# A state-space layer mixed with a feed-forward layer: first loads dealt anew to two queues, six first blocks begun with one row group, x's columns 256 to 447 in one load

## The chip, the cores and the metric

One core of a Trainium2 chip runs the whole program. The metric is device time in microseconds (us). Three runs of the kernel before gave 136.68, 136.72 and 136.97 us, so the median is 136.72. One more execution was recorded by the hardware profiler; it took 136.32 us, of which 134.8 lie between its first and its last instruction (the span). All rows of profiles in this text count from the start of that span.

The engines are TensorE (PE, with its weight loads as PEld), VectorE (DVE), ScalarE (ACT), GpSimd (POOL) and SyncE (SP). SyncE computes nothing here; it issues transfers. ScalarE issues transfers too, in its own queue, between its other instructions. Each engine works through its own instructions in the order in which they were written, and waits on semaphores for others.

## What is computed

```python
x = A_x                                                     # 2048 x 448, bf16
g = sigmoid((x * gate_w).sum(-1, keepdims=True))
# a: a diagonal complex state space with 448 states
Lam_bar = exp(dt * Lam)
Bu = einsum("bld,pd->blp", x, ((Lam_bar - 1) / Lam)[:, None] * Bmat)
h[t] = Lam_bar * h[t - 1] + Bu[t]
a = 2 * einsum("blp,dp->bld", h, Cmat).real + x * Dskip
# b: a feed-forward layer, 448 -> 1792 -> 448
b = silu(x @ w1) @ w2
out = g * a + (1 - g) * b
```

Only the first 9 us or so concern this change: the part of `x @ w1` for the first quarter of the rows.

## The kernel before

**Rows and tiles.** Two neighbouring rows of x are one row of a view `x2` with 1024 rows of 896 columns: columns 0 to 447 are the even row, 448 to 895 the odd one. The work on rows is in four chunks of 512: even rows of the first and second half, then odd rows. Each chunk of `x @ w1` has 14 blocks of 128 columns of w1, and the 448 of the contraction are cut into three parts of 128 (`j` = 0, 1, 2) and a remainder of 64. TensorE needs x transposed, with the contraction along the partitions: that is the tile `XT`, and `XR` holds a copy of a remainder in the other half of the partitions.

**The first chunk is special.** All other chunks are transposed by the transfer engines. The first one, rows 0 to 511 of `x2`, is loaded as it lies into `XH` (a view of the tile `XN`), in four row groups of 128 rows (`k` = 0 to 3), and TensorE transposes it by multiplying with the identity (`turn_k`, line 493; `turn_x` does two row groups). The result stands in a bank of PSUM, and VectorE copies it into `XT` (`turned_k` for one row group, line 503; `turned_x` for two or all four, line 509). The bank of each `j` is in `PB = (6, 7, 6, 7)`; for `j` = 0 the row groups use bank 6, 5, 6 and 7.

**Loads.** Lines 275 to 294 issue them. Columns 0 to 255 of the four row groups are four loads (`XA0` to `XA3`, 64 KB each). W1's first part (`j` = 0, the first 768 columns of w1) is two loads of 384 columns (`W1Ej00`, `W1Ej01`, 96 KB each), the second and third part one load of 192 KB each (`W1Ej1`, `W1Ej2`). Columns 256 to 383 and 384 to 511 of all four row groups are two loads of 128 KB (`XB0`, `XB1`); of the second, the last 64 columns belong already to the odd rows. The order in the queues is:

| place | SyncE's queue | ScalarE's queue |
|---|---|---|
| 1 | x, row group 0 | x, row group 1 |
| 2 | W1 first part, columns 0 to 383 | W1 first part, columns 384 to 767 |
| 3 | x, row group 2 | x, row group 3 |
| 4 | W1 second part | Lambda_im |
| 5, 6 | log_dt, Lambda_re | x columns 256 to 383; W1 third part |
| 7 | x columns 384 to 511 | (an activation table is loaded) |
| then | W1's remainder and later columns | W1's remainder and later columns |

**The order on TensorE.** It starts with 20 matmuls on constants (`warm`, line 483). Then come the transposes of row groups 0 and 1, and the generator `ffn1_first` (line 424), which computes six blocks (0, 2, 4, 1, 3, 5; even blocks need only the first half of W1's first part) for `j` = 0, 1 and 2 in six banks. It gives up control at each `yield`, and the lines around line 518 put the transposes in these places:

1. three even blocks with row group 0 alone (128 columns, line 427), then the same with row group 1 (line 435);
2. transposes of row groups 2 and 3, `j` = 0;
3. three odd blocks with row groups 0 and 1 (256 columns); transposes of row groups 2 and 3 for `j` = 1;
4. six blocks with row groups 2 and 3 (256 columns); three blocks for `j` = 1 (512 columns);
5. four tiny matmuls that turn the parameter rows into columns (`mm_cols`, line 474);
6. the four transposes for `j` = 2 into bank 6, which VectorE copies out in one piece; three blocks for `j` = 1;
7. the four transposes for the last columns into bank 7; six blocks for `j` = 2;
8. the remainders (`ffn1_rem`, line 449), two blocks side by side in the two halves of the array, each followed by a Silu on ScalarE (line 457).

After it the dense part runs to the end, mainly lines 362, 816, 801 and 1054.

**Who waits for whom.** `Tracker` keeps for each name (such as `ps6` for bank 6, or `XB0`) the last writer and the readers since. A reader waits for the last writer; a writer waits for the last writer and for all readers. A bank is one name, whatever part of it is used:

```python
        for b in writes:
            st = self.state(b)
            if st.w is not None:
                add(*st.w)
            for key, value in st.r.items():
                add(key, value)
```

**On VectorE and ScalarE in this time.** VectorE copies transposes out (lines 503, 509, 573), copies the parameter columns (line 530) and computes decays and phases in small steps (lines 558 to 584); from 10 us on it builds phases (lines 614, 616, 621), spreads two broadcast rows (`GD`, line 672), copies a remainder (line 241) and rearranges B (lines 680, 682). ScalarE computes two exponentials of the parameters (line 564), the second of them from a product that VectorE makes after its copy of `j` = 2; then it loads the table for Silu (line 574) and starts the Silus.

Of the kernel before, what the change touches and what calls it, by code (L numbers as in the profile page):

```python
# [11 lines left out]
BF16 = DT.bfloat16  # L12
# [7 lines left out]
D = 448  # L20
# [130 lines left out]
def gated_mix(nc, A_x, A_Lambda_re, A_Lambda_im, A_B_re, A_B_im, A_C_re, A_C_im, A_log_dt,  # L151
              A_Dskip, B_x, B_w1, B_w2, gate_w, out):
    with ExitStack() as ctx:
        E = ctx.enter_context
        T = Tracker(nc, ctx)
# [15 lines left out]
        XR = sb("XR", [128, NK], BF16)  # L171
# [4 lines left out]
        XN = sb("XN", [128, 2 * NKT * D], BF16)  # L176
# [12 lines left out]
        ID = sb("ID", [128, 128], BF16)  # L189
# [31 lines left out]
        ps = E(nc.psum_tensor("ps", [128, 8, 512], F32))  # L221
# [3 lines left out]
        def ld(eng, dst, src, key, group=None):  # L225
            return T.dma(eng, lambda e: e.dma_start(dst, src), writes=[key], group=group)  # L226
# [2 lines left out]
            return T.dma("sp", lambda e: e.dma_start_transpose(dst, src), reads=reads,  # L229
                         writes=[key, *also], group=group)  # L230

        XE = [(["XTe000", "XTe001", "XTe010", "XTe011", "XTe02"], ["XTe03"]), (["XTe1"], ["XTer1"])]
        XO = [([f"XTo{h}"], [f"XTr{h}"]) for h in range(2)]

        def swap_xr(eng, h, odd):
            hs = slice(h * 512, (h + 1) * 512)
            if odd:
                T.op(eng, lambda e: e.tensor_copy(XR[0:64, hs], XT[64:128, 7, hs]), reads=XO[h][1],
                     writes=[f"XR{h}b"])
            else:  # L240
                T.op(eng, lambda e: e.tensor_copy(XR[64:128, hs], XT[0:64, 3, hs]), reads=XE[h][1],
                     writes=[f"XR{h}a"])
# [8 lines left out]
            return v.rearrange("(o n) -> o n", o=1)  # L251

        XH = XN[:, 0:8 * D].rearrange("p (k c) -> p k c", k=4)
        XA = ["XA0", "XA1", "XA2", "XA3", "XB0", "XB1"]
        FA, FB = 768, 1280
        x0 = x2[0:512, 0:512].rearrange("(k p) c -> p k c", p=128)

        def ld_w(eng, j, f0=0, f1=FA, key=""):
            ld(eng, W1E[:, j, f0:f1], B_w1[j * 128:(j + 1) * 128, f0:f1], f"W1Ej{j}{key}")
# [12 lines left out]
                          B_w1[384:448, FA:].rearrange("p (n c f) -> p n c f", n=2, c=2)[:, :, c, :], f"W1Es{c}")  # L272
            return ld(eng, W1E[p, 3, 0:384], B_w1[384:448, 384 * c:384 * c + 384], f"W1Er{c}")

        for k, eng in enumerate(("sp", "act")):
            ld(eng, XH[:, k, 0:256], x0[:, k, 0:256], XA[k])
        for c, eng in enumerate(("sp", "act")):
            ld_w(eng, 0, 384 * c, 384 * c + 384, c)
        for k, eng in ((2, "sp"), (3, "act")):
            ld(eng, XH[:, k, 0:256], x0[:, k, 0:256], XA[k])  # L280
        ld_w("sp", 1)
        for i, (eng, v) in enumerate((("sp", A_log_dt), ("sp", A_Lambda_re), ("act", A_Lambda_im))):
            ld_row(eng, i, v)
        for i, eng in enumerate(("act", "sp")):
            ld(eng, XH[:, :, 256 + 128 * i:384 + 128 * i], x0[:, :, 256 + 128 * i:384 + 128 * i], XA[4 + i])
        ld_w("act", 2)
        T.op("act", lambda e: e.activation(JK[:, 0:1], HP[:, :], AF.Exp), reads=["HP"], writes=["JK0"])
        gE = [ld_wr(eng, c, False) for c, eng in enumerate(("sp", "act"))]
        ld_w3("sp", 0, 2, FA, FB, "d")
# [8 lines left out]
            ld("act", dst[0:32, :], row(src).partition_broadcast(32).rearrange("p o n -> p (o n)"), key)  # L298

        def load_xn(h):  # L300
            c0 = 0 if h else 512
            ld("sp", XN[:, 8 * h * D:8 * (h + 1) * D].rearrange("p (k c) -> p k c", k=4)[:, :, c0:],
               x2[h * 512:(h + 1) * 512, c0:].rearrange("(k p) c -> p k c", p=128), f"XN{h}")

# [5 lines left out]
        for i, src in enumerate((A_B_re, A_B_im)):  # L310
# [15 lines left out]
             writes=["IOTA"])  # L326
# [19 lines left out]
        def rem_keys(odd, h, p):  # L346
            return (XO if odd else XE)[h][1] if (p is UP) == bool(odd) else [f"XR{h}{'b' if odd else 'a'}"]

# [74 lines left out]

        def ffn1_first():
            banks = [nxt() for _ in range(NF1)]
            for fb in (0, 2, 4):
                T.op("pe", lambda pe, fb=fb, bank=banks[fb]: pe.matmul(
                    ps[:, bank, 0:128], W1E[:, 0, ff(fb) * 128:(ff(fb) + 1) * 128], XT[:, 0, 0:128],
                    start=True, stop=True), reads=["W1Ej00", "XTe000a"], writes=[f"ps{banks[fb]}"])
            for j, h in ((0, 0), (0, 1), (1, None), (2, None)):  # L430
                for n, fb in enumerate((0, 2, 4, 1, 3, 5)):
                    k = h == 0 and n < 3
                    c = slice(0, 512) if h is None else slice(128 if k else 256 * h, 256 * h + 256)
                    bank = banks[fb]
                    T.op("pe", lambda pe, fb=fb, bank=bank, j=j, h=h, c=c, k=k: pe.matmul(  # L435
                        ps[:, bank, c], W1E[:, j, ff(fb) * 128:(ff(fb) + 1) * 128], XT[:, j, c],
                        start=(h == 0 and not k), stop=(h == 0 and not k), skip_group_check=(h != 0 or k)),
                        reads=[f"W1Ej{j}" if j else f"W1Ej0{fb % 2}"] + (
                            ["XTe02"] if j == 2 else [f"XTe0{j}{h}"] if h is not None else [f"XTe0{j}0", f"XTe0{j}1"]),
                        writes=[f"ps{bank}"])  # L440
                    if (j, h, n) in ((0, 0, 2), (0, 0, 5), (1, None, 2), (1, None, 5)):
                        yield
            yield banks

# [34 lines left out]
        def warm(n, b):  # L479
            def mm(pe):  # L480
                ins = None
                for _ in range(n):
                    ins = pe.matmul(ps[:, b, 0:128], ones, ones, start=True, stop=True)
                return ins
            T.op("pe", mm, writes=[f"ps{b}"])
# [3 lines left out]
        xp = [ps[:, b, 0:256].bitcast(BF16) for b in PB]  # L489

        def turn_k(j, k, b=None):
            b = PB[j] if b is None else b
            T.op("pe", lambda pe: pe.transpose(  # L493
                ps[:, b, 0:256].bitcast(BF16)[:, k * 128:(k + 1) * 128], XH[:, k, j * 128:(j + 1) * 128], ID[:, :]),
                reads=[XA[k if j < 2 else 2 + j], "ID"], writes=[f"ps{b}"])

        def turn_x(j, i):
            for k in (2 * i, 2 * i + 1):
                turn_k(j, k)
# [6 lines left out]
        def turned_x(j, i=None, b=None):  # L506
            c, key = (slice(0, 512), f"XTe0{j}") if i is None else (slice(256 * i, 256 * i + 256), f"XTe0{j}{i}")
            b = PB[j] if b is None else b
            T.op("dve", lambda e: e.tensor_copy(XT[:, j, c], ps[:, b, 0:256].bitcast(BF16)[:, c]),
                 reads=[f"ps{b}"], writes=[key])  # L510

        for k in range(2):
            turn_k(0, k, 6 - k)
            turned_k(0, k, 6 - k)
        turn_x(1, 0)
        turned_x(1, 0)
        warm(1, 4)
        first = ffn1_first()
        next(first)
        for k in (2, 3):  # L520
# [3 lines left out]
        for k in (2, 3):  # L524
# [5 lines left out]
        T.op("dve", lambda e: e.tensor_copy(  # L530
            PV[:, :, :], ps[:, 7, 256:288].rearrange("p (t c) -> p t c", c=8)[:, :, 0:4]),
            reads=["pv", "ps7"], writes=["PV"])
        for i in range(2):
            turn_x(2, i)
        turned_x(2)
        next(first)
        for i in range(2):
            turn_x(3, i)
# [8 lines left out]
        def col(n):  # L547
            i = pc(n)
            return P[:, i, :]
# [13 lines left out]
        def pact(o, a, f, ra, scale=1.0, bias=0.0):  # L563
# [5 lines left out]
            col("phf"), LIM, 1.0 / TWO_PI, col("dt"), ALU.mult, ALU.mult), reads=["PV", "dt"], writes=["phf"])  # L569
        ptt("ar", col("dt"), LRE, ALU.mult, ["dt", "PV"])  # L570
        pact("mag", col("ar"), AF.Exp, ["ar"])
        turned_x(3)
        T.op("dve", lambda e: e.tensor_copy(XR[64:128, 0:512], xp[3][0:64, :]), reads=["ps7"], writes=["XR0a"])
        T.op("act", lambda e: e.activation(JK[:, 0:1], HP[:, :], AF.Silu), reads=["HP"], writes=["JK0"])
        ld_b(GWB, gate_w, "GW")
        ld_b(DB, A_Dskip, "DB")
# [9 lines left out]
            reads=["f2"] + SGN, writes=["f2s"])  # L586
        first = next(first)
# [54 lines left out]
        def xblock(b):  # L642
            v = XN[:, 4 * b * D:4 * (b + 1) * D].rearrange("p (k c) -> p k c", k=4) if b > 1 else \
                XH[:, :, b * D:(b + 1) * D]
            return v, [*(XA if b < 2 else []), *([f"XN{b // 2}"] if b else [])]

        def block(tile):
            return tile // 4 if tile > 7 else tile % 2
# [19 lines left out]

        phases(0)
        phases(2, "dve")  # L670
        for n in (32, 64):
            T.op("dve", lambda e, n=n: e.tensor_copy(GD[n:2 * n, :, :], GD[0:n, :, :]), reads=["GW", "DB"],
                 writes=["GW", "DB"])
        phases2(0)
        decays()
        swap_xr("dve", 1, 0)
        phases2(2)
        phases(3)
        phases(1, "dve")
# [1 line left out]
             writes=["BTz"] + BTK[2:4])  # L681
# [486 lines left out]
        f = ffn1(2)  # L1168
# [100 lines left out]
```

## Time and profile before

| | us |
|---|---|
| median of three runs | 136.72 |
| the profiled execution | 136.32 |
| its span | 134.8 |
| TensorE busy in the span | 131.4 |
| VectorE | 115.5 |
| ScalarE | 93.7 |
| GpSimd | 15.9 |
| transfer engines, share of 16, from 0.8 to 4.0 / 4.0 to 6.6 / 6.6 to 9.3 | 0.62 / 0.93 / 1.03 |

The page's 40 slices are 3.37 us each, so the change lies in the first three of them:

```profile
PE   7899999999999999999999999999999999999993
DVE  1379999917999798999999999999999999994554
ACT  0469698899939999769999597796124337879200
POOL 7109358550000000000000000000000000000000
DMA  3999959996994310000211000000000000222123
```

Each digit is the busy share of one slice in tenths. Issuing a transfer is not counted as busy. The waits of TensorE before 14 us, by what ended them (time in all, how often, longest):

```profile
PE ps L427 <- DMA W1E<-in_B_w_dram: 0.4, 1, 0.4
```

On the weight loads there are three more: 0.6 us for the same load, 0.3 us in two pieces for the loads of x (line 493), and 0.2 us for a copy by VectorE (line 503).

### The profile page before, as it was taken

The page shows a single profiled execution, that of the slowest core. Times are in us where ns is not written, and L with a number is a line of the kernel's source. Part 1 is how long each engine was busy: PE and PEld are TensorE (multiplying, and loading weights), DVE is VectorE, ACT ScalarE, POOL GpSimd, SP SyncE. Part 2 cuts the span into 40 slices and gives each one's busy share as a digit, 9 for nine tenths or more (in the row PEclk, how much of TensorE's full clock was granted, in tenths as well). Part 3 has the DMA queues.
Part 4 walks back from the last instruction along what each step waited for, and adds up shares of the span by engine and source line. Part 5 has one row for each costly group of instructions (what it writes and reads, how often), then busy time and mean ns, then how long its engine had stood idle before and what let it go on. Part 6 is the DMA issues. An engine that isn't in the chain of part 4 may idle for free.

```text
span 134.8 us, 2637 instructions
## 1 busy us (share of the span) xinstructions
PE 131.4 (97%) x1074; PEld 65.7 (49%) x1075; DVE 115.5 (86%) x154; ACT 93.7 (70%) x146; POOL 15.9 (12%) x32
## 2 busy tenths in 40 slices
PE   7899999999999999999999999999999999999993
PEld 7544444444444554444445544445555555555552
DVE  1379999917999798999999999999999999994554
ACT  0469698899939999769999597796124337879200
POOL 7109358550000000000000000000000000000000
DMA  3999959996994310000211000000000000222123
GB/s 103 258 284 191 181 129 220 179 379 182 264 188 98 71 46 0 0 0 5 66 45 45 5 0 0 0 5 0 0 0 0 0 0 15 92 94 76 68 81 124
DMA packets 25248, 11.78 MB, mean 87 GB/s; under 512 B 17619, under 2 KB 24726, under 8 KB 25238
## 3 DMA queue, kind: packets, MB, share of 16 engines
q1 hardware_dynamic: 23252, 10.47, 33.4%
q10 hardware_dynamic: 1986, 1.17, 3.0%
q8 instruction: 8, 0.13, 0.4%
q14 instruction: 2, 0.02, 0.0%
HBM read 5.34 MB, written 1.84 MB: 53 GB/s over the span
## 4 chain that ended last, share of the span: by engine, by line
PE 93%; DMA 3%; ACTq 1%; DVE 1%; issue 0%
PE ps L362 44%; PE ps L801 16%; PE ps L816 16%; PE ps L1054 15%; DMA XN<-in_A_x_dram 3%; PE ps L435 1%; ACTq L226 1%; DVE TMPS L1078 1%; PE ps L449 1%; PE ps L493 0%
## 5 line engine op out<-in xcount | busy, mean ns | idle before, releaser
L362 PE MATMUL ps<-XT,W1E 64*128 64x512 bf16 x325 | 41.4, 376 | 0.0
L457 ACT ACTIVATE AT<-ps 128x1024 bf16<-128x1024 f32 x28 | 28.2, 1019 | 7.4 <-PE ps L362 7.2
L362 PEld LDWEIGHTS ps<-XT,W1E 64*128 64x128 bf16 x325 | 16.9, 94 | 19.0 <-ACT AT L457 0.3
L362 PE MATMUL ps<-XT,BT 64*128 64x512 bf16 x156 | 22.4, 377 | 0.0
L816 PE MATMUL ps<-W,AT 64*128 64x448 bf16 x224 | 21.5, 349 | 0.0
L801 PE MATMUL ps<-W,AT 128*128 128x448 bf16 x112 | 21.4, 353 | 0.0
L816 PEld LDWEIGHTS ps<-W,AT 64*128 64x128 bf16 x224 | 10.9, 94 | 10.4
L801 PEld LDWEIGHTS ps<-W,AT 128*128 128x128 bf16 x112 | 10.9, 98 | 10.5 <-issue 0.4
L845 ACT ACTIVATE BT<-ps,GT 128x448 bf16<-128x448 f32 x8 | 5.1, 633 | 13.2 <-PE ps L801 13.2
L901 DVE SCALAR_TENSOR_TENSOR HS<-VE,P,ps 128x512 bf16<-128x512 bf16 (+1 forms) x13 | 9.6, 780 | 3.8 <-PE ps L362 3.8
L362 PEld LDWEIGHTS ps<-XT,BT 64*128 64x128 bf16 x156 | 8.1, 94 | 9.3 <-DVE HS L901 0.4
L945 DVE TENSOR_TENSOR_SCAN G<-P,Q 128x1024 f32<-128x1024 f32 (+1 forms) x6 | 11.4, 1922 | 0.0
L1054 PE MATMUL ps<-CO,VE 128*128 128x448 bf16 (+2 forms) x63 | 11.1, 332 | 0.0
L1054 PE MATMUL ps<-CO,HS 128*128 128x448 bf16 x56 | 11.1, 353 | 0.0
L362 PE MATMUL ps<-XR,W1E 64*128 64x512 bf16 x25 | 9.3, 376 | 0.0
L1054 PEld LDWEIGHTS ps<-CO,VE 128*128 128x128 bf16 x63 | 6.0, 98 | 4.8
L1054 PEld LDWEIGHTS ps<-CO,HS 128*128 128x128 bf16 x56 | 5.5, 98 | 5.1
L898 DVE TENSOR_TENSOR Q<-G,COS 128x2048 bf16<-128x2048 f32 (+1 forms) x4 | 7.0, 1756 | 0.1
L898 DVE TENSOR_TENSOR Q<-G,SIN 128x2048 bf16<-128x2048 f32 (+1 forms) x4 | 7.0, 1751 | 0.0
L863 ACT ACTIVATE VE<-ps 128x1024 bf16<-128x1024 f32 x6 | 6.1, 1019 | 1.2 <-PE ps L362 1.2
L865 ACT ACTIVATE ps<-VE,P 128x1024 f32<-128x1024 bf16 x6 | 6.7, 1118 | 0.2
L901 DVE SCALAR_TENSOR_TENSOR VE<-HS,P,FP 128x512 bf16<-128x512 bf16 (+1 forms) x7 | 6.6, 977 | 0.1
(126 smaller groups left out, 181.2 us busy)
## 6 DMA issues: line engine op xcount, KB each, us to landing
W<-in_B_w_dram SPq DMA_DIRECT2D x2, 784.0 KB, 5.9
XN<-in_A_x_dram SPq DMA_DIRECT2D x1, 896.0 KB, 5.3
out_dram<-OT SPq DMA_DIRECT2D x8, 112.0 KB, 1.7
out_dram<-TMPS SPq DMA_DIRECT2D x7, 112.0 KB, 1.7
HS<-HS SPq DMA_DIRECT2D x4, 128.0 KB, 2.3
XN<-in_A_x_dram SPq DMA_DIRECT2D x1, 384.0 KB, 3.8
W1E<-in_B_w_dram SPq DMA_DIRECT2D x1, 256.0 KB, 5.0
W1E<-in_B_w_dram ACTq DMA_DIRECT2D x1, 256.0 KB, 5.3
```

The costliest lines, as they stand in the source:

```text
L226: return T.dma(eng, lambda e: e.dma_start(dst, src), writes=[key], group=group)
L362: ins = pe.matmul(ps[:, bank, :], w(p, j), xh(odd, h, j, p), start=start and j == js[0], stop=stop and j == js[-1], skip_group_check=seeded)
L457: T.op("act", lambda e: e.activation(a[:, fb:fb + n, :], ps[:, bank:bank + n, :], AF.Silu), reads=[f"ps{bank + i}" for i in range(n)], wri ...
L801: ins = pe.matmul(ps[:, bank, 0:D], a[:, fb, q * 128:(q + 1) * 128], W2[:, ff(fb), :], start=(first and fb == 0), stop=(fb == NFB - 1), sk ...
L816: ins = pe.matmul(ps[:, bank, 0:D], a[p, fb, q * 128:(q + 1) * 128], W2[p, ff(fb), :], start=(start and fb == 0), stop=(not start and fb = ...
L845: T.op("act", lambda e: e.activation(bs(tile), ps[:, bank, 0:D], AF.Copy, scale=sc), reads=[f"ps{bank}", "GT2" if h else "GRI"], writes=ks)
L863: T.op("act", lambda e: e.activation(VE[:, m:m + 2, hs], ps[:, b[0]:b[0] + 2, :], AF.Copy), reads=[f"ps{i}" for i in b], writes=vs)
L865: T.op("act", lambda e: e.activation(ps[:, o[0]:o[0] + 2, :], VE[:, m:m + 2, hs], AF.Copy, scale=c1("lr", pt)), reads=vs + ["lr"], writes= ...
L898: T.op("dve", lambda e: e.tensor_tensor(o, a, b, op), reads=reads, writes=writes)
L901: T.op("dve", lambda e: e.scalar_tensor_tensor(o, a, s, b, ALU.mult, ALU.add), reads=reads, writes=writes)
L945: T.op("dve", lambda e: e.tensor_tensor_scan(G[:, c, w], rb, Q1[:, c, w], init, ALU.mult, ALU.add), reads=[f"Q1{c}", "rr", f"G{c}"], write ...
L1054: ins = pe.matmul(ps[:, bank, c], state(kt, odd, m), CO[:, m, c], start=False, stop=(m == YB[-1]), skip_group_check=True)
```

## The change

It does seven things.

1. Both halves of W1's first part are issued on ScalarE's queue, in places 1 and 2; row groups 0, 1 and 2 of x are places 1 to 3 of SyncE's. Row group 3 stays at place 3 of ScalarE's.
2. Columns 256 to 447 of the four row groups are one load of 192 KB on ScalarE's queue, named `XB` (`XA[4]`), where the load of columns 256 to 383 was. W1's third part moves to SyncE's queue, to the place of the former second load. The 64 columns of odd rows that this load no longer brings come with the later load of that half (`load_xn(0)`, 448 columns instead of 384).
3. The last part's transposes take columns 320 to 447, so that the remainder stands in partitions 64 to 127 of the bank; two copies of 64 partitions bring it to both places.
4. `ffn1_first` begins all six blocks with row group 0, then all six with row group 1, 128 columns each.
5. Row groups 0 and 1 are transposed for `j` = 0 and `j` = 1 as each arrives, with two matmuls on constants in between (one before, after both).
6. For `j` = 1 one block more comes ahead of the transposes for `j` = 2, and these are copied out in two pieces, each after two transposes.
7. On VectorE the first phase step and the copy of the remainder come ahead of the two copies of `GD`.

```diff
-        XA = ["XA0", "XA1", "XA2", "XA3", "XB0", "XB1"]
+        XA = ["XA0", "XA1", "XA2", "XA3", "XB"]
-        x0 = x2[0:512, 0:512].rearrange("(k p) c -> p k c", p=128)
+        x0 = x2[0:512, 0:D].rearrange("(k p) c -> p k c", p=128)
...
-        for k, eng in enumerate(("sp", "act")):
-            ld(eng, XH[:, k, 0:256], x0[:, k, 0:256], XA[k])
-        for c, eng in enumerate(("sp", "act")):
-            ld_w(eng, 0, 384 * c, 384 * c + 384, c)
+        for i in range(2):
+            ld("sp", XH[:, i, 0:256], x0[:, i, 0:256], XA[i])
+            ld_w("act", 0, 384 * i, 384 * i + 384, i)
         for k, eng in ((2, "sp"), (3, "act")):
             ld(eng, XH[:, k, 0:256], x0[:, k, 0:256], XA[k])
         ld_w("sp", 1)
...
-        for i, eng in enumerate(("act", "sp")):
-            ld(eng, XH[:, :, 256 + 128 * i:384 + 128 * i], x0[:, :, 256 + 128 * i:384 + 128 * i], XA[4 + i])
-        ld_w("act", 2)
+        ld("act", XH[:, :, 256:D], x0[:, :, 256:D], XA[4])
+        ld_w("sp", 2)
...
-            c0 = 0 if h else 512
+            c0 = 0 if h else D
...
-            for fb in (0, 2, 4):
+            for fb in (0, 2, 4, 1, 3, 5):
...
-                    start=True, stop=True), reads=["W1Ej00", "XTe000a"], writes=[f"ps{banks[fb]}"])
+                    start=True, stop=True), reads=[f"W1Ej0{fb % 2}", "XTe000a"], writes=[f"ps{banks[fb]}"])
...
-                    k = h == 0 and n < 3
+                    k = h == 0
...
-                    if (j, h, n) in ((0, 0, 2), (0, 0, 5), (1, None, 2), (1, None, 5)):
+                    if (j, h, n) in ((0, 0, 2), (0, 0, 5), (1, None, 2), (1, None, 3), (1, None, 5)):
                         yield
...
             b = PB[j] if b is None else b
+            c = min(j * 128, D - 128)
...
         for k in range(2):
             turn_k(0, k, 6 - k)
             turned_k(0, k, 6 - k)
-        turn_x(1, 0)
+            turn_k(1, k)
+            if k == 0:
+                warm(2, 4)
         turned_x(1, 0)
-        warm(1, 4)
...
+        next(first)
         for i in range(2):
             turn_x(2, i)
-        turned_x(2)
+            turned_x(2, i)
         next(first)
...
-        turned_x(3)
-        T.op("dve", lambda e: e.tensor_copy(XR[64:128, 0:512], xp[3][0:64, :]), reads=["ps7"], writes=["XR0a"])
+        for b, key in ((XT[0:64, 3, 0:512], "XTe03"), (XR[64:128, 0:512], "XR0a")):
+            T.op("dve", lambda e, b=b: e.tensor_copy(b, xp[3][64:128, :]), reads=["ps7"], writes=[key])
...
         phases(0)
         phases(2, "dve")
+        phases2(0)
+        swap_xr("dve", 1, 0)
         for n in (32, 64):
             T.op("dve", lambda e, n=n: e.tensor_copy(GD[n:2 * n, :, :], GD[0:n, :, :]), reads=["GW", "DB"],
                  writes=["GW", "DB"])
-        phases2(0)
         decays()
-        swap_xr("dve", 1, 0)
```

More of the change, by code (lines that the diff above doesn't have):

```diff
@@ L230, in ldt @@
                          writes=[key, *also], group=group)
-        XE = [(["XTe000", "XTe001", "XTe010", "XTe011", "XTe02"], ["XTe03"]), (["XTe1"], ["XTer1"])]
+        XE = [(["XTe000", "XTe001", "XTe010", "XTe011", "XTe020", "XTe021"], ["XTe03"]), (["XTe1"], ["XTer1"])]
         XO = [([f"XTo{h}"], [f"XTr{h}"]) for h in range(2)]
@@ L438, in ffn1_first @@
                         reads=[f"W1Ej{j}" if j else f"W1Ej0{fb % 2}"] + (
-                            ["XTe02"] if j == 2 else [f"XTe0{j}{h}"] if h is not None else [f"XTe0{j}0", f"XTe0{j}1"]),
+                            ["XTe020", "XTe021"] if j == 2 else [f"XTe0{j}{h}"] if h is not None else [f"XTe0{j}0", f"XTe0{j}1"]),
                         writes=[f"ps{bank}"])
-                    if (j, h, n) in ((0, 0, 2), (0, 0, 5), (1, None, 2), (1, None, 5)):
+                    if (j, h, n) in ((0, 0, 2), (0, 0, 5), (1, None, 2), (1, None, 3), (1, None, 5)):
                         yield
@@ L492, in turn_k @@
             b = PB[j] if b is None else b
+            c = min(j * 128, D - 128)
             T.op("pe", lambda pe: pe.transpose(
-                ps[:, b, 0:256].bitcast(BF16)[:, k * 128:(k + 1) * 128], XH[:, k, j * 128:(j + 1) * 128], ID[:, :]),
-                reads=[XA[k if j < 2 else 2 + j], "ID"], writes=[f"ps{b}"])
+                ps[:, b, 0:256].bitcast(BF16)[:, k * 128:(k + 1) * 128], XH[:, k, c:c + 128], ID[:, :]),
+                reads=[XA[k if j < 2 else 4], "ID"], writes=[f"ps{b}"])
         def turn_x(j, i):
@@ L644, in xblock @@
                 XH[:, :, b * D:(b + 1) * D]
-            return v, [*(XA if b < 2 else []), *([f"XN{b // 2}"] if b else [])]
+            return v, XA if b == 0 else [f"XN{b // 2}"]
         def block(tile):
```

## The prediction

> **What bounds the kernel now.** I read first the table of busy time by stretch, to learn whether an earlier start is worth anything at the end. Its columns are the stretch in us, its length, and the busy time and count of PE, weight loads, DVE, ACT and POOL.
>
> ```profile
> 0.80:4.00 3.20, 2.83 (x25) 2.56 (x25) 1.00 (x7) 0.24 (x1) 2.81 (x7) 1.00 0.62 161
> ...
> 6.60:9.30 2.70, 2.54 (x21) 1.27 (x18) 1.83 (x8) 1.64 (x3) 0.00 (x0) 1.00 1.03 298
> 9.30:90.00 80.70, 80.70 (x777) 37.62 (x776) 74.18 (x89) 70.12 (x106) 12.71 (x20) 1.00 0.46 98
> 90.00:132.30 42.30, 42.30 (x231) 22.12 (x228) 36.85 (x46) 20.49 (x37) 0.00 (x0) 1.00 0.12 39
> ```
>
> From 9.3 us on TensorE is busy for all of every stretch. So the moment at which the remainder matmuls of line 449 start (9.31) fixes the end: what that moment gains or loses, the span of 134.8 gains or loses, as long as no new wait appears behind it.
>
> Second, the chain of waits, in order of time: what leads to line 449.
>
> ```profile
> 2.77 4.00 DMA XN<-in_A_x_dram
> 6.77 0.05 issue
> 6.82 0.40 PE ps L493 x4
> 7.21 0.05 issue
> 7.27 0.59 PE ps L435 x2
> 7.86 0.22 PE ps L493 x4
> 8.08 1.29 PE ps L435 x6
> 9.38 0.75 PE ps L449 x6
> 10.13 31.76 PE ps L362 x294
> ```
>
> The chain passes through one load: x's columns 256 to 383, issued on ScalarE's queue at 2.77, landed at 6.77. Behind it TensorE works without a break.
>
> Third, the timeline of the same time: what TensorE did before that load landed, and how long it idled for it.
>
> ```profile
> 4.49 0.34 PE L493 MATMUL ps<-ID,XN 128*128 128x128 bf16 x2
> ...
> 4.75 0.36 DVE L503 COPY XT<-ps 128x128 bf16<-128x128 bf16 x2 [0.88 <-PE ps L493]
> ...
> 5.16 1.48 PE L435 MATMUL ps<-XT,W1E 128*128 128x256 bf16 x9
> ...
> 6.47 0.24 PE L474 MATMUL ps<-ID,R 128*128 128x4 bf16 x4
> ...
> 6.81 0.23 PEld L493 LDWEIGHTS ps<-ID,XN 128*128 128x128 bf16 x4 [0.19 <-DMA XN<-in_A_x_dram]
> 6.82 0.40 PE L493 MATMUL ps<-ID,XN 128*128 128x128 bf16 x4
> 7.25 0.42 DVE L509 COPY XT<-ps 128x512 bf16<-128x512 bf16 x1 [0.32 <-PE ps L493]
> ```
>
> The four small matmuls of line 474 are streamed by about 6.58 (6.47 plus four at 0.028); the transposes start at 6.82. Some 0.24 us of idle time is all that this wait costs. Before it, the six 256-column matmuls that begin at 5.16 wait for row group 3: its load lands at 4.5 (issued 1.72, 2.8 to landing), is transposed, and VectorE copies it out by 5.11.
>
> **The change, part by part.** From start-to-start times here: a warm transpose takes 0.056 us, a 256-column matmul 0.11, a 512-column one 0.215.
>
> *Early loads and first blocks.* Both halves of W1's first block go on ScalarE's queue (0.78 and 1.24, landing before at 1.24 + 2.7 and 1.24 + 2.9), row groups 0 to 2 on SyncE's, row group 3 stays third on ScalarE's. The first matmul can start near 3.6, where it starts now at 4.01. The three 128-column matmuls of odd blocks and three more now stand ahead of the transposes of row groups 2 and 3; they replace three of 256 columns, so the sum of columns is the same. What follows is bound elsewhere: the six 256-column matmuls cannot start until row group 3 has landed plus 0.6 (5.16 - 4.5). Its queue now carries 192 KB ahead of it instead of 160; SyncE's carries 192 KB up to row group 2 instead of 224, and W1's second block then competes sooner. Bounds: 0.2 earlier, since 192 KB of x come with no W1 between them on SyncE's queue and the two landings there now (2.8 and 4.3) lie far apart, or 0.3 later (32 KB more on its own queue and as much from the other, at the 257 GB/s of the stretch from 4.0 to 6.6). I take no shift, start 5.16, range 4.95 to 5.45. From there the order of work up to the wait for columns 256 and on is 0.66 (six of 256) + 0.65 (three of 512) + 0.11 (line 474) + 0.22, since one 512-column matmul more is moved ahead of the wait: 1.64. TensorE is there at 6.80 (6.59 to 7.09).
>
> The row: the 20 warm-up matmuls fill 0.82 to 2.90, 0.105 apart, the same size takes 0.056 at 6.82; what is pulled ahead of about 4.3 runs at half pace. The Trainium skill, "TensorE: Matmul & The Clock Gate", section "Part 1: The HAM clock gate", puts the same down to a gate that opens after some 3.4 us of activity, in a free-running window, and so speaks against this part. By the row a start 0.4 earlier at 4.01 would be worth 0.2 of warm work; by the rule a window that ends later makes it less and changes from run to run.
>
> *Columns 256 to 447 as one load.* 192 KB instead of two of 128 KB, in 512 rows of 384 B, issued at the same place on ScalarE's queue (2.77). No row shows such a load. Nearest: the old load on the same place, same number of rows, took 4.0; its twin on SyncE's queue 4.2; W1's third block, the same 192 KB, 4.5 from 3.21; W1's second block, 192 KB, 3.4 from 2.17. So 6.2 to 7.3; by the nearest, 4.1, it lands at 6.87. W1's third block moves to SyncE's queue, where it is issued at 3.3 instead of 3.21; even at 4.5 it lands at 7.8, and its first use is at 8.3 below. The remaining W1 loads on ScalarE's queue are issued a slot (0.5) earlier; the closest of them (issued 4.43, 5.1 to landing) is first used at 9.97, so an earlier landing brings nothing and one 0.4 later would still be covered. The later x load takes 448 instead of 384 columns; its first reader in VectorE's order is at 25.9.
>
> The Trainium skill, "DMA: Bandwidth & Descriptors", section "Specifications", gives 512 B as the least transfer for full rate. By that rule the 384 B rows are still short ones and 192 KB of them should land later than 128 KB did; by the queue's rows alone the load may come as early as 6.2.
>
> *The copies of columns 256 to 383 in halves: a new wait.* Now four transposes into bank 6 are followed by one copy. After: two transposes, a copy of 256 columns, two transposes, a copy. A write to a bank waits for the copy that reads it, and both halves use bank 6, so the third transpose waits for VectorE. Behind it on TensorE stand the two remaining 512-column matmuls, the four transposes of the last columns, the six last matmuls and all the rest. Price: the second transpose starts 0.056 after the first; the old copy started 0.26 after the start of the transpose that released it (6.99 to 7.25); a 256-column copy takes 0.29 (line 509 at 3.58); TensorE resumes 0.05 after (5.11 to 5.16). 0.66 from the first transpose to the third, where 0.11 were work: 0.55 idle.
>
> From the first transpose to line 449, before: 4 x 0.056 + 3 x 0.215 + 4 x 0.056 + 6 x 0.215 + 0.10 for the change of tile size = 2.49 (6.82 to 9.31). After: 0.66 + 2 x 0.056 + 2 x 0.215 + 4 x 0.056 + 6 x 0.215 + 0.10 = 2.81. The second copy is out at 1.27, before the six matmuls at 1.42: no second stall.
>
> *The sum.* First transpose at the later of 6.80 and 6.87 + 0.05 = 6.92; line 449 at 9.73; 0.42 later than 9.31.
>
> *Edits with no cost of their own.* The split copies of the last columns (two of 64 rows) replace one of 128 and one of 64 rows at 0.42 each; they end 2.52 after the first transpose, line 449 needs them at 2.71. ScalarE's exponential and table load hang behind the second half copy: released at 1.27 instead of 0.86, the table stands 0.1 ahead of the first Silu (0.17 now); without that cover each 0.1 costs 0.1, since the matmuls at 10.83 wait for that Silu. On VectorE the two GD copies (2.40) move behind one phase step and the copy that waits for a transposed load (14.8): POOL's step that it needs ends at 13.37 + 0.42 = 13.8, then 1.23 for the phase step, 0.3, 2.4 and 0.5 for the small decay operations: 18.2, where the next phase step starts at 16.91 now, 1.3 later. The first reader on TensorE of what follows is the XR and BT pair at 22.70; the copy of line 680 ends at 20.68, so there are 2.0 of cover, of which 1.3 - 0.4 = 0.9 is used; without it 0.9 would be lost. Behind lies 3.20 of VectorE idle time before line 901 at 30.55, which takes up the delay.
>
> Span 134.8 + 0.42 = 135.2; the profiled execution's 136.32 would be 136.74. The median of the runs shown is 136.72, 0.4 above that execution, and I add the difference to it: 137.14.
>
> **Rivals.** *The front gains as much as the stall costs.* The point of balance is a first transpose at 6.50. It takes row group 3 some 0.25 earlier and the joined load with the 3.4 of W1's second block (6.2). For it: 64 KB less ahead of W1's third block, and x's first groups undisturbed. Against: queue place and row count unchanged. First transpose 6.55: 136.8. *The front gains more:* it must stand at 6.23 or before, so the load by 6.18 and row group 3 by 4.0; then 9.04, or 136.4. *The reorder on VectorE decides:* it does once the copy of line 680 falls 1.1 further behind, which takes a transposed load of the swap (issued 10.12, landed 14.8) or a POOL step that is as much later; each 0.1 beyond costs 0.1 on top of the stall, so about 137.5 at 1.5. Against: nothing ahead of it became slower. *The joined load takes as long as W1's third block,* 4.5: first transpose 7.32, line 449 at 10.13 instead of 9.31, 137.5; the slow end of the forecast.
>
> **How the numbers follow.** 0.2% is 0.27 us, what a measurement of this kernel can tell. Forecast (half copies stall TensorE, 136.8 to 137.6): 0.70, of it 0.08 below 136.99. Balanced front: 0.13. Front gains more: 0.11. VectorE: 0.06. Faster 0.11; within 0.2%: 0.08 + 0.13 = 0.21; slower 0.62 + 0.06 = 0.68. Its own range: 136.85 to 137.5. Leaving out the quick front and little else: 136.7 to 137.6. The time is the forecast's, 137.1.
>
> **What would show it.** A gap of about 0.5 us between second and third transpose of columns 256 to 383, ended by VectorE's copy; the joined load landing near 6.9; the six 256-column matmuls starting near 5.16 although the first matmul starts before 4.0; the remainder matmuls near 9.7; TensorE without idle time after. Wrong if that start is at 9.3 or before, or if TensorE idles near 23.

## The result, and the profile after

The changed kernel takes 137.25 us (median of 22 runs, 136.79 to 139.21), the kernel before, run beside it, 136.72 (22 runs, 135.98 to 137.58). The ratio is 1.004, interval 1.0025 to 1.0055: 0.34 to 0.75 us slower. Single runs of 138.4 to 139.5 us came up in 9 of 102 runs of the kernels here that have the new dealing of the loads, and in none of 159 runs of those with the old; the ratios leave out the six of them over 139, but not three of 138.4 to 138.6 in f3 below.

The profiled execution of the changed kernel took 136.89 us, its span is 135.5. First its chain of waits in order of time (start, length, what), from the transposes of row groups 2 and 3 for `j` = 1 on:

```profile
5.48 0.19 PE ps L492 x2
5.68 0.87 PE ps L433 x7
...
7.30 0.13 PE ps L492 x2
7.42 0.02 issue
7.45 0.30 DVE XT L508
7.75 0.05 issue
7.79 0.29 PE ps L492 x2
8.08 0.43 PE ps L433 x2
8.51 0.22 PE ps L492 x4
8.73 1.29 PE ps L433 x6
10.03 0.75 PE ps L447 x6
```

Lines 492, 433 and 447 are the former 493, 435 and 449. The load of x's columns 256 and on, which took 4.00 us of the chain before, is gone from it. A copy by VectorE (line 508) stands in the middle of the transposes instead. The timeline gives the exact starts:

```profile
3.71 0.80 PE L425 MATMUL ps<-XT,W1E 128*128 128x128 bf16 x6
...
5.49 1.49 PE L433 MATMUL ps<-XT,W1E 128*128 128x256 bf16 x8
...
7.13 0.27 PE L492 MATMUL ps<-ID,XN 128*128 128x128 bf16 x2
7.79 0.29 PE L492 MATMUL ps<-ID,XN 128*128 128x128 bf16 x2 [0.39 <-DVE XT L508]
...
9.96 0.39 PE L447 MATMUL ps<-XT,W1E 64*128 64x512 bf16 x1
```

The third transpose starts 0.66 after the first, where 0.11 were work. (Nine matmuls run from 5.49 to 7.13, six of 256 columns and three of 512; the profile lacks the record of one.) The load of row group 3, issued at 1.72 before and 1.71 after, took longer to land, first before, then after:

```profile
DMA to landing us min/median/max: 2.8/2.8/2.8
DMA to landing us min/median/max: 3.1/3.1/3.1
```

The remainder starts at 9.96 instead of 9.31. After it the busy table (stretch, length, then busy time and count of PE, weight loads, DVE, ACT, POOL) is full as it was before:

```profile
6.60:9.96 3.36, 2.97 (x22) 1.43 (x22) 1.99 (x9) 1.56 (x3) 0.00 (x0) 1.00 0.98 266
9.96:90.00 80.04, 80.04 (x771) 37.41 (x772) 72.74 (x88) 69.61 (x105) 13.68 (x20) 1.00 0.45 97
90.00:132.95 42.95, 42.95 (x237) 22.32 (x233) 37.52 (x47) 21.09 (x38) 0.00 (x0) 1.00 0.11 38
```

So the whole difference lies ahead of the remainder. In all fourteen profiles of this study the profiled time is the remainder's start plus 126.9 to 127.1 us, which lets one read the other.

### The profile page after: what moved, and what is told of

Read it like the earlier page. It is cut to its first block, busy times and chain, and to the rows that moved or that the text cites. A ratio compares the mean times of both kernels' runs of the same rounds, so it can differ in the third digit from the quotient of the medians.

```text
span 135.5 us, 2642 instructions
## 1 busy us (share of the span) xinstructions
PE 132.2 (98%) x1078; PEld 66.2 (49%) x1079; DVE 115.0 (85%) x155; ACT 93.7 (69%) x146; POOL 16.8 (12%) x32
## 4 chain that ended last, share of the span: by engine, by line
PE 97%; DVE 1%; issue 0%
PE ps L360 44%; PE ps L802 16%; PE ps L817 16%; PE ps L1055 15%; PE ps L433 3%; PE ps L481 2%; PE ps L492 1%; DVE TMPS L1079 1%; PE ps L447 1%; PE ps L425 0%; DVE XT L508 0%; PE ps L472 0%
```

## The experiments

The runs e1 to e4, f1 to f4 and g0 to g3 were made on one chip each, and the kernel before ran beside them each time: medians 136.38, 136.44 and 136.50. Intervals of a ratio are 0.002 to 0.003 to each side, or 0.25 to 0.4 us, so single differences between two experiments decide little. What the fourteen profiles show ahead of the remainder (us; rows 2 and 3 are landings of row groups, "pace" is when the matmuls begin to start twice as close together as at first, "six" the start of the six 256-column matmuls on rows 2 and 3, "turn" the first transpose of columns 256 to 383, "gap" from its second to its third, less the 0.06 of one):

| kernel | row 2 | row 3 | pace | six | turn | gap | remainder |
|---|---|---|---|---|---|---|---|
| before | 4.35 | 4.55 | 4.3 | 5.16 | 6.82 | 0.00 | 9.31 |
| g3, one matmul ahead | 4.03 | 4.21 | 6.2 | 5.40 | 7.41 | 0.00 | 9.79 |
| f2, halves alone | 4.20 | 4.41 | 4.0 | 5.00 | 6.42 | 0.55 | 9.46 |
| e3, changed, old dealing | 4.12 | 4.28 | 5.1 to 5.2 | 5.37 | 7.31 | 0.55 | 10.13 |
| f4, changed, old dealing, one copy | 4.41 | 4.59 | 6.2 | 5.36 | 7.39 | 0.00 | 9.77 |
| changed | 4.15 | 4.83 | 5.5 | 5.49 | 7.13 | 0.55 | 9.96 |
| f1, changed again | 4.52 | 4.69 | 6.8 | 5.47 | 7.72 | 0.55 | 10.55 |
| e4, changed, old VectorE order | 4.74 | 4.91 | 4.3 | 5.51 | 7.14 | 0.55 | 9.97 |
| g2, changed, gaps filled | 4.72 | 5.44 | 5.7 | 6.09 | 7.73 | 0.55 | 10.55 |
| e1, changed, one copy | 5.06 | 5.23 | 4.6 to 5.3 | 5.83 | 7.46 | 0.00 | 9.84 |
| e2, changed, two banks | 5.25 | 5.42 | 4.6 to 5.5 | 6.02 | 7.65 | 0.08 | 10.01 |
| f3, dealing alone | 4.82 | 5.00 | 6.5 | 5.98 | 7.63 | 0.00 | 10.12 |
| g0, dealing alone again | 4.28 | 4.48 | 7.1 | 5.76 | 7.84 | 0.00 | 10.52 |
| g1, dealing alone, gaps filled | 5.01 | 5.17 | 4.5 | 5.77 | 7.19 | 0.00 | 9.67 |

Two things set "six". In eight profiles it stands 0.59 to 0.66 after the landing of row group 3. In the other six (g3, e3, f4, f1, f3, g0) it stands 0.77 to 1.28 after it: there TensorE was still at half pace when the rows came, and its own work ahead of the six took that much longer.

### Undoing one part: the stall (e1, e2), the dealing (e3), VectorE's order (e4)

**e1**, one copy for columns 256 to 383:

```diff
         for i in range(2):
             turn_x(2, i)
-            turned_x(2, i)
+        T.op("dve", lambda e: e.tensor_copy(XT[:, 2, 0:512], xp[2]), reads=["ps6"], writes=["XTe020", "XTe021"])
```

> The changed kernel, but the four transposes of columns 256 to 383 are again copied out in one piece. Theory (the third transpose's wait for the first half copy costs 0.55 us of TensorE time, one for one): the gap before the third transpose is gone, from the first of these transposes to the remainder matmuls it is 2.83 - 0.55 = 2.28 us, and the time is 0.5 below the changed kernel, about 136.7, the same as before. Rival (the loss comes from the newly dealt loads, the stall only takes the place of another wait, such as the Silu table): less than 0.2 below the changed kernel.

137.07 us (136.57 to 137.36, 12 runs), ratio 1.0046, interval 1.0026 to 1.0067. In the timeline the four transposes are one group again, and the remainder follows the first of them by 2.38 instead of 2.83:

```profile
7.46 0.39 PE L492 MATMUL ps<-ID,XN 128*128 128x128 bf16 x4
...
7.88 0.42 DVE L536 COPY XT<-ps 128x512 bf16<-128x512 bf16 x1 [0.29 <-PE ps L492]
...
8.46 1.45 PE L433 MATMUL ps<-XT,W1E 128*128 128x512 bf16 x6
...
9.84 0.39 PE L447 MATMUL ps<-XT,W1E 64*128 64x512 bf16 x1
```

The gap went as it should, but 2.28 was expected. Most of the rest is a new wait: the six last matmuls need the one copy, which is out at 8.30, and start at 8.46, 0.12 later than the transposes before them allow. f4 and g3, the other kernels with one copy and one matmul moved ahead, have the same 0.12, and no other kernel has it. So the matmul that is moved ahead is missing behind, where it covered the copy; the halves remove that wait of 0.12 and bring the one of 0.55. The time did not follow: against before, e1 is no better than the changed kernel. In this profile row group 3 landed 0.40 later than in the changed kernel's.

**e2**, two halves in two banks:

```diff
-        PB = (6, 7, 6, 7)
+        PB = (6, 7, 6, 6)
...
-        for i in range(2):
-            turn_x(2, i)
-            turned_x(2, i)
+        for k in range(4):
+            turn_k(2, k, 6 + k // 2)
+        for i in range(2):
+            turned_x(2, i, 6 + i)
...
-            T.op("dve", lambda e, b=b: e.tensor_copy(b, xp[3][64:128, :]), reads=["ps7"], writes=[key])
+            T.op("dve", lambda e, b=b: e.tensor_copy(b, xp[3][64:128, :]), reads=["ps6"], writes=[key])
```

> The changed kernel with its two half copies, but the second half's transposes go into bank 7 and the last columns' into bank 6, so that no transpose waits for the first half copy. Theory (it is the shared bank, not the cutting into halves, that costs): 0.45 to 0.5 below the changed kernel, since only a wait of some 0.08 for the copy of the parameter columns is left. Rival (two short copies on VectorE cost more than one, whatever the bank): no better than 137.1.

136.97 us (136.35 to 137.24, 12 runs), ratio 1.0027, interval 1.0009 to 1.0045. The gap is 0.08, and the four transposes take 0.48 where they took 0.39 in e1:

```profile
7.65 0.48 PE L492 MATMUL ps<-ID,XN 128*128 128x128 bf16 x4
```

So it is the shared bank that makes the wait. The time is 0.18 below the changed kernel's by the ratios, less than was expected, and the intervals overlap.

**e3**, the first four loads dealt as before:

```diff
-        for i in range(2):
-            ld("sp", XH[:, i, 0:256], x0[:, i, 0:256], XA[i])
-            ld_w("act", 0, 384 * i, 384 * i + 384, i)
+        for k, eng in enumerate(("sp", "act")):
+            ld(eng, XH[:, k, 0:256], x0[:, k, 0:256], XA[k])
+        for c, eng in enumerate(("sp", "act")):
+            ld_w(eng, 0, 384 * c, 384 * c + 384, c)
```

> The changed kernel with the first four loads dealt to the queues as before (row group 1 and W1's second half on ScalarE's queue, W1's first half on SyncE's), all else as changed. Theory (the first transpose of columns 256 to 383 stands at the landing of row group 3 plus 2.3 us, and the new dealing lands row group 3 some 0.3 later): row group 3 lands near 4.55, that transpose starts near 6.85 instead of 7.13, and the time is 0.2 to 0.3 below the changed kernel. Rival (the dealing is neutral; the late start of 7.13 comes from a TensorE clock that opened late in that one execution): no difference, row group 3 lands near 4.8.

136.87 us (136.37 to 137.46, 12 runs), ratio 1.0028, interval 1.0009 to 1.0047. Row group 3 lands at 4.28, 0.55 earlier than in the changed kernel, but the six matmuls start only 0.12 earlier, at 5.37: TensorE itself, which starts the first blocks at 3.67 and runs them at half pace until about 5.2, comes no sooner. W1's second part then lands late (6.28) and makes TensorE wait 0.30. So an earlier first transpose isn't seen in this one profile (7.31 against 7.13). By the ratios the time is 0.16 below the changed kernel's; the intervals overlap here too.

**e4**, VectorE's order of before (the phase step and the copy of the remainder behind the two `GD` copies):

```diff
-        phases2(0)
-        swap_xr("dve", 1, 0)
         for n in (32, 64):
...
+        phases2(0)
         decays()
+        swap_xr("dve", 1, 0)
```

> The changed kernel with VectorE's old order (the two copies of the broadcast rows ahead of the phase step, the decays and the copy of the remainder). Theory (the order there is covered): the same as the changed kernel within 0.1. Rival (the reorder decides): 0.3 or more below it.

137.32 us (136.90 to 137.87, 9 runs), ratio 1.007, interval 1.0044 to 1.0095. Undoing the reorder brings nothing. The ratio is 0.4 us above the changed kernel's, where 0.1 was expected; the intervals overlap. From the remainder's start to TensorE's end it is 123.46 us here, in the changed kernel and in the kernel before: the reorder is covered. On this chip e4 has the dealing and the stall, e1 the dealing, e3 the stall: 0.95, 0.63 and 0.38 us over before. There they nearly add.

### One part alone on the kernel before

**f1**, the changed kernel once more, as the partner of the next three.

> The changed kernel as it is, to stand beside the others on one chip, and for a second profile of it. Theory now (two losses: row group 3 lands 0.3 to 0.9 later from a few of the 16 transfer engines, and the third transpose waits 0.55): row group 3 lands between 4.8 and 5.4, the gap before the third transpose is 0.55, the time is 0.5 to 0.8 above the kernel before. Rival (the late landing was chance in four profiles): it lands near 4.5.

137.22 us (136.92 to 139.51, 11 runs), ratio 1.0044, interval 1.0025 to 1.0063. The profiled execution took 137.48 us, 0.59 more than the first of the same kernel, and its timeline shows where:

```profile
5.47 2.10 PE L433 MATMUL ps<-XT,W1E 128*128 128x256 bf16 x8
...
7.72 0.27 PE L492 MATMUL ps<-ID,XN 128*128 128x128 bf16 x2
8.38 0.29 PE L492 MATMUL ps<-ID,XN 128*128 128x128 bf16 x2 [0.39 <-DVE XT L508]
```

The eight matmuls start at the same time as in the first profile (5.47 and 5.49) but take 2.10 instead of 1.49. The six of 256 columns start 0.214 apart, where 0.11 is usual. The stall is the same 0.55. Row group 3 landed at 4.69, between the expectation (4.8 to 5.4) and its rival (4.5).

**f2**, the copy in halves alone, on the kernel before (its names of the two halves go with it):

```diff
         for i in range(2):
             turn_x(2, i)
-        turned_x(2)
+            turned_x(2, i)
```

> The kernel before with one edit alone: the four transposes of columns 256 to 383 are copied out in two halves. Theory (the stall costs one for one): a gap of 0.55 before the third transpose, and 0.55 above the kernel before, ratio 1.004. Rival (the stall only takes the place of another wait): less than 0.2 above.

137.15 us (136.57 to 137.45, 12 runs), ratio 1.0043, interval 1.0025 to 1.0061. Its chain of waits:

```profile
6.57 0.02 issue
6.60 0.17 DVE PV L530
6.77 0.26 DVE XT L509
7.03 0.04 issue
7.08 0.28 PE ps L493 x2
```

The wait arises on the kernel before as well. Here the half copy also stands behind the copy of the parameter columns (line 530), and 3.04 pass from the first transpose to the remainder, 0.55 more than before. The runs give 0.34 to 0.83 us: the stall alone costs what its gap says.

**f3**, the new dealing alone on the kernel before (e3's diff the other way round).

> The kernel before with one edit alone: the first loads dealt anew (both halves of W1's first part on ScalarE's queue, row groups 0 to 2 on SyncE's). Theory (the dealing itself lands row groups 2 and 3 later, and they start the six 256-column matmuls): row group 3 lands at 4.8 to 5.4, the six matmuls start 0.6 after it, the time is 0.2 to 0.6 above the kernel before. Rival (the landing is bound by the sum of bytes, not by the dealing): row group 3 lands near 4.5 and the time is within 0.2 of before.

137.29 us (136.81 to 139.07, 12 runs), ratio 1.0072, interval 1.0042 to 1.0102. Four of its runs are over 138; the median of the other eight is 137.12, still 0.7 above before. Its chain of waits goes through a load that no chain with the old dealing has, row group 2:

```profile
1.70 3.13 DMA XN<-in_A_x_dram
4.82 0.05 issue
4.87 0.47 PE ps L492 x2
5.34 0.64 PE ps L434 x3
5.98 0.21 PE ps L492 x2
```

Issued at 1.70, it lands at 4.82, where it landed at 4.35 before. TensorE idles 0.43 us at 3.5 and 0.32 at 4.9 in this profile (distance between two starts, less the usual 0.107). The dealing alone makes the kernel before slower. The landing is only one part of that in this profile: the six start 0.98 after it, at half pace.

**f4**, the changed kernel with the old dealing and one copy (the diffs of e1 and e3 together): what is left are the order of the first blocks, the joined load, the matmul moved ahead, the split last copies and the reorder.

> The changed kernel with both suspects undone: the old dealing of the first four loads and one copy for columns 256 to 383. What is left of the change is the joined load of columns 256 to 447, six blocks begun with one row group, one matmul more ahead of the wait, and VectorE's order. Theory: the gap of 0.55 is gone, row group 3 lands near 4.4, the remainder matmuls start between 9.1 and 9.4, the time is that of the kernel before or up to 0.2 below. Rival (what is left costs as well): 0.2 or more above the kernel before.

136.72 us (136.37 to 137.19, 12 runs), ratio 1.0015, interval 0.9999 to 1.0031. With both parts undone nearly all of the loss is gone. The rest of the change gains nothing either. In the profile the remainder starts at 9.77, not at 9.1 to 9.4 as expected: TensorE was at half pace until 6.2, and the wait of 0.12 for the one copy is there too.

### Idle pieces, and one matmul ahead

**g0**, f3's kernel again, as the partner of g1.

> The kernel before with the new dealing of the first four loads alone, once more, as the partner of the next kernel on the same chip. Before: 5 of its 12 runs lay between 138.3 and 139.1 us, which no run with the old dealing reached. Expected: again at least 2 runs over 138.0, median 0.5 to 1.0 us over the kernel before.

137.21 us (136.63 to 137.56, 6 runs), ratio 1.006, interval 1.0037 to 1.0084. (The count in the expectation is wrong: four of f3's runs were over 138, a fifth was 137.73.) None of the six runs is over 138. Its profile doesn't show the late rows: row group 3 landed at 4.48, as early as before, and still the remainder starts at 10.52.

```profile
5.76 2.13 PE L434 MATMUL ps<-XT,W1E 128*128 128x256 bf16 x9
...
8.06 0.81 PE L434 MATMUL ps<-XT,W1E 128*128 128x512 bf16 x3
8.89 0.40 PE L492 MATMUL ps<-ID,XN 128*128 128x128 bf16 x4
```

The nine matmuls take 2.13 instead of 1.48, since the half pace lasted until 7.1, and the load of x's columns 384 and on landed at 8.85 instead of 7.48, for which TensorE idled 0.19. In the changed kernel these columns come with the joined load, landed at 6.48.

**g1**, the same with TensorE's idle pieces filled:

```diff
+            if k == 0:
+                warm(4, 4)
...
         next(first)
+        warm(3, 7)
```

> The same, with seven matmuls on constants where TensorE idled for row groups: four after row group 0's transposes and three ahead of row group 2's. Theory (TensorE's idle pieces of 0.43 and 0.37 us at 3.5 and 4.9 make the clock open one window later in some runs): no run over 138.0, median 0.0 to 0.3 us below its partner. Rival (transfers that land late in some runs make the long runs): as many runs over 138.0 as its partner has, same median, or up to 0.1 more.

137.06 us (136.57 to 137.33, 10 runs), ratio 1.0038, interval 1.0016 to 1.0061. None over 138, but its partner had none either: of the long runs this says nothing. The median is 0.15 lower, within the intervals. In its profile the half pace ended at 4.5, the fill leaves TensorE 0.29 idle ahead of row group 2, and the six start 0.60 after a late row group 3 (5.17). By the ratio the kernel still takes 0.2 to 0.8 us more than before.

**g2**, the changed kernel with `warm(3, 7)` ahead of row group 2's transposes.

> The changed kernel with three matmuls on constants ahead of row group 2's transposes. Theory of the late clock: no run over 138.0 (the changed kernel has had some up to 139.5), median within 0.2 us of 137.2, the stall in columns 256 to 383 still there (0.55). Rival (late landings): runs over 138.0 remain.

137.02 us (136.76 to 139.29, 8 runs), ratio 1.0047, interval 1.0024 to 1.007. One run of 139.29 remains, against the theory that idle pieces alone make the long runs. But the profile, of another run, still shows 0.33 idle: its chain has row group 3 where f3's had row group 2,

```profile
1.71 3.73 DMA XN<-in_A_x_dram
5.44 0.05 issue
5.49 0.29 PE ps L492
```

landed at 5.44, the latest of all. The fill came between row group 1's work and row group 2, not here. What makes the long runs stays open.

**g3**, the kernel before with one 512-column matmul more ahead of the wait for columns 256 to 383:

```diff
-                    if (j, h, n) in ((0, 0, 2), (0, 0, 5), (1, None, 2), (1, None, 5)):
+                    if (j, h, n) in ((0, 0, 2), (0, 0, 5), (1, None, 2), (1, None, 3), (1, None, 5)):
...
+        next(first)
         for i in range(2):
             turn_x(2, i)
```

> The kernel before with one edit of the change alone: one 512-column matmul more ahead of the wait for columns 256 to 383. Theory (TensorE idles some 0.24 us for that load, and work put there is free): 0.1 to 0.2 us faster than before, the wait in the profile down to 0.05 or less. Rival (in most runs the clock opens later than in the first profile, so TensorE arrives after the load anyway): within 0.1 us of before.

136.38 us (136.02 to 136.95, 12 runs), ratio 0.9993, interval 0.9975 to 1.0011: not told apart from before. In its profile the load landed at 6.13, long before TensorE came to it:

```profile
5.40 1.85 PE L435 MATMUL ps<-XT,W1E 128*128 128x256 bf16 x9
...
7.41 0.39 PE L493 MATMUL ps<-ID,XN 128*128 128x128 bf16 x4
```

Nine 256-column matmuls of the same kind took 1.48 in the profile of before. With the slow pace lasting to 6.2 there is no idle time for that load to fill. And the 0.12 for the one copy (see e1) would take back part of any gain. No kernel tried beats the kernel before.

## Why the prediction held, and where its sum was off

**Held: the stall.** A gap of 0.55 between the second and third transpose was forecast, from a shared bank. It is 0.55 in every profile with half copies into one bank, 0.08 with two banks, and f2 shows its cost alone. From the first transpose to the remainder 2.81 was forecast, 2.83 came.

**Held: the remainder's start fixes the end.** TensorE has no new idle time behind it.

**Failed: "I take no shift".** The six 256-column matmuls were to start at 5.16, within 4.95 to 5.45; they start at 5.49. In nine profiles with the new dealing row group 3 lands at 4.48 to 5.44, mean 5.02; in five with the old at 4.21 to 4.59, mean 4.41. The bound was worked out from the bytes ahead in the queue (0.3 later at most). In the changed kernel's first profile row group 3 lands 0.28 later, at the bound's edge; on the mean it is 0.6, and row group 2 loses as much as row group 3 (mean 4.73 against 4.22), though its own queue carries less ahead of it than before. So the early W1 halves (3.15 and 3.59 instead of 3.97 and 4.16) go with later landings of the loads that the path needs next. That the dealing alone costs time is shown by f3 and g0: 0.5 to 1.4 us by the ratios, 0.7 by the medians without the long runs. How much of it is the late landing is argued, not shown: in e1, e2, e4, g1, g2 and the first profile of the changed kernel the six follow the landing by 0.60 to 0.66, but in f1, f3 and g0 the half pace of TensorE holds them up, and g1, which fills idle pieces, gains less than the intervals can tell. What in the engines' service of the two queues delays the rows was not isolated.

**Right direction, wrong reason: the first transpose.** 6.92 was forecast, set by the joined load at 6.87. That load landed at 6.48, in 3.7 us, and decided nothing; TensorE came at 5.49 + 1.64 = 7.13, just past the range given for it (6.59 to 7.09). The 1.64 itself was exact. The joined load of 192 KB took 3.4 to 4.0 us in eight profiles (mean 3.70), the load of 128 KB in its place 3.1 to 4.0 in six (mean 3.44). The rival in which the joined load needs 4.5 us is out in every profile.

**The sum.** The forecast's 0.42 was the stall's 0.32 and 0.10 for the load. Measured is 0.55 by the ratio: the late rows take the load's place, and with 0.31 they weigh three times as much in the first profile (7.13 against 6.82). That the time came so near is therefore partly luck: a term that was put at nothing replaced one that did not arise.

Two losses of 0.6 (f2) and some 0.7 us (f3, g0) on the kernel before nevertheless make only 0.55 (0.60 in f1) together. Why they don't add there is not shown. The new order of the first blocks may account for some of it: with the dealing alone TensorE idles 0.43 and 0.32 us for rows in f3, where the changed kernel's first profile has 0.14 (at 4.87) and works on the odd blocks instead. But e1, with the same order and row group 2 landing at 5.06, idles 0.46, and it lost 0.63. That was not tried by itself. For the rest, e1 and e2 removed the gap, but only e2 came out below the changed kernel (by 0.0013 of the ratio, inside the intervals), while e4 beside them on the same chip stands 0.3 to 0.6 above both. Whether the stall costs its full 0.45 within the changed kernel is therefore not settled by the times.

**VectorE.** The reorder was to be covered, with 0.9 of 2.0 us used. It is covered. The next phase step came at 17.70, 0.8 later than before, where 1.3 was worked out: the `GD` copies took 0.81 together in their new place, not 2.40.

**The rivals.** *Front balances* and *front gains more* needed row group 3 earlier; it came later. *VectorE decides* needed a late POOL step; one came (below), and was covered.

## What to carry to other kernels

Where one name stands for a whole bank, as here, a copy cut in two lets the next work start early only if the halves lie in different banks; otherwise the producer of the second half waits for the first copy, here 0.55 us on the engine that sets the end. Work that is moved ahead to fill one wait is missing where it stood: here it uncovered 0.12 us of the copy. Before a load is moved ahead, look up which load the path waits for after it, and read that one's landing in several profiles, not in bytes per queue. And where a kernel's first microseconds matter, profile the same kernel twice: tenths of a microsecond in one profile may belong to the execution and not to the change.

## What the runs showed of the hardware

**The pace of TensorE doubles at a moment that varies.** 128-column matmuls start 0.107 us apart at first and 0.056 later, 256-column ones 0.214 and 0.11. The change comes near 4.3 us in the profile of before, 5.5 in that of the changed kernel, 6.2 in g3 and f4, 6.8 in f1; the earliest is 4.0 (f2), the latest 7.1 (g0), all with TensorE at work since 0.82, but for short idle pieces. The granted clock is given as 1.00 throughout, so only the distances show it. The two profiles of the changed kernel differ by 0.61 us in the pieces shown and by 0.59 us in their times. The prediction's base, the profile of before, was an early one; that may be why its time lay 0.4 us under the median, which the prediction added. The Trainium skill, "TensorE: Matmul & The Clock Gate", section "Part 1: The HAM clock gate", tells of a gate with a free-running window, so that the moment isn't tied to the kernel's start. That it moves from run to run here agrees with this; the 500 ns to either side that the page gives for it do not, since here it lies between 3.2 and 6.3 us after TensorE began.

**A VectorE step and a GpSimd step can exclude each other.** From the timeline of the changed kernel:

```profile
14.05 1.23 DVE L622 SCALAR_TENSOR_TENSOR FP<-G,FP 128x1024 f32<-128x1024 f32 x1 [0.94 <-POOL G L617]
...
14.19 2.08 POOL L615 TENSOR_SCALAR Q<-IOTA,P 128x1024 f32<-128x1024 f32 x1 [0.17 <-POOL G L617]
...
15.31 1.10 DVE L241 COPY XR<-XT 64x512 bf16<-64x512 bf16 x1
...
16.45 0.81 DVE L675 COPY GD<-GD 32x896 bf16<-32x896 bf16 x2
```

The GpSimd step took 1.12 us before; here it takes 2.08, ending 1.0 after VectorE's step. Meanwhile VectorE's small copy, 0.29 before, takes 1.10 and ends 0.14 after GpSimd's. The `GD` copies run at 0.4 each when GpSimd is idle and took 1.2 each beside it before. The Trainium skill, "SBUF — State Buffer", section "Who interferes with whom", describes a port pair that one of the two engines holds for a whole instruction while the other blocks; these rows agree with it.
